# A new order of steps, loads and casts in a fused sigmoid-attention and token-mixing kernel, with more of the q/k exchange on GpSimd and idle tiled matmuls on TensorE

## The chip, the cores and the metric

The kernel runs on one core of a Trainium2 chip. The metric is device time in microseconds (us) of one execution, lower is better. A profile is one further execution recorded by the hardware profiler; its span runs from the first to the last instruction.

## The reference

Eight batches, 12 heads, sequence 448, head size 64. Sigmoid attention, then a token-mixing MLP on its output:

```python
scores = q @ k.T / sqrt(64) - log(448)        # per batch and head, 448 x 448
x = sigmoid(scores) @ v                       # heads side by side: 448 x 768 per batch
wq, wk = x @ w_q, x @ w_k                     # 448 x 64 each
W_tok = (wq @ wk.T) / sqrt(64)                # 448 x 448
out = relu(W_tok @ x) @ w_out                 # 448 x 768 per batch, float32
```

Inputs and output are float32 in device memory; the kernel computes in bf16 with float32 accumulation. It forms W_tok @ x as wq @ (wk.T @ x).

## The kernel before

**Quads.** Four heads of one batch are a quad; there are 24, three to a batch. A quad takes 7 score steps and 7 value steps. A score step (letter S, lines 299 to 310) is four 64x64-tiled matmuls into a pair of PSUM banks, then one sigmoid of 128x896 on ScalarE (line 308) which frees the pair. A value step (P or p, line 321) is four tiled matmuls into a pair that the quad keeps for all 7; after the last, VectorE (P) or ScalarE (p) copies it to `xt`. There are four bank pairs in all, handed out in the order in which they were given back.

**The MLP.** x and X transpose `xt` to `xn` on TensorE (tiled, line 361, or whole, line 344); W, w, L, l project with `w_q | w_k`: W and w as one full-array matmul (line 400), L and l as four tiled ones (line 387), whose two halves VectorE then has to copy and add (lines 394, 395); N transposes `wk`; U, u (line 431, full rows) and T, t (line 447, tiled, with an extra add at 452) form wk.T @ x; M, m form the mix and its ReLU; O, o and I, i are the output projection. Four steps make 128 rows of output. For batches 2 to 5 O is tiled (line 516); for the others O is a full-array matmul (line 600) and I its tiled form (line 556), whose halves VectorE adds (line 562).

**The order.** It is written out by hand in two strings. `PLAN` gives the steps one letter each; instructions are emitted in that order, and every engine works through its own in that order. `ORDER` gives the loads (`q7` is q of quad 7, `w3` the third row block of the output weights), issued on SP as one of six load buffers comes free, that is when the tensor six places earlier has been cast. Each is cast float32 to bf16: on GpSimd in the sequence of `ORDER`, or, where it has a dot, on VectorE, at the earliest 9 scores after its load was issued (4 in the first quads).

**How q and k get their layout.** The letter that `PLAN` gives to a quad's q sets it:

- q, k and a, b: TensorE transposes into a bank pair, VectorE copies out (lines 212, 220, 286, 291).
- c, d: the cast (line 188) writes an order in which six GpSimd copies of 32 partitions exchange quarter blocks (`arrange`, lines 157, 160, 163, one shared `swap` tile), then VectorE transposes 128 partitions, once for q and once for k (line 259).
- r, s, z: no exchange; VectorE transposes 128 partitions twice (line 252) and then four times 32 partitions (line 228, `quadrants`).
- e, f, g: exchanged as for c, plus two more VectorE transposes (line 263) and four small DMAs (line 240, `move`).

At most two quads of the c, r or e kind hold a cast buffer at once. F is a full-array matmul on zeros that nothing reads (line 814).

Of the kernel before, what the change touches and what calls it, by code (L numbers as in the profile page):

```python
# [17 lines left out]
def kernel(  # L18
# [12 lines left out]
    nc = tc.nc  # L31
    B, H, S, HD = q.shape
# [4 lines left out]
    NI, NP = 7, 64  # L37
# [4 lines left out]
    HALF = (slice(0, 64), slice(64, 128))  # L42
# [23 lines left out]
    pairs = [banks[:, 2 * n : 2 * n + 2] for n in range(4)]  # L66
    pairs16 = [banks16[:, 2 * n : 2 * n + 2] for n in range(4)]
    free2 = [0, 1, 2, 3]
# [29 lines left out]
    zeros = singles.tile([P, 512], BF16)  # L98
# [21 lines left out]
    def xt(u, j):  # L120
# [4 lines left out]


    PLAN = (
        "FSSFSKFSSqFSFSkFSpFSpSqpPpPSPSSkFSpPSFSSabSrPSPSPXSsPSPpPSpp"
        "PpSPSXSwwSSzWWXwWSPPpSPppNSPSqkSXSSpUSPSpMpSPpPSqkSSPSpPMSPP"
        "PPSSWWXSSwWWWSPpcPSdMpSPPPSXSNSxSqkSUSpPSMppSppPSOoSMSOOqSkS"  # L130
        "oOSMrPpSppPSPSPOoSSsSOzXOSCLlLSLSLLSpPPPPcpPSSdOOSOSCNxSOScU"
        "SPPSPdprPSPPSPPsPPPSpSOPSXoSxSzooSCMLlCSLllLSPcpPSPPPPSCSOdX"
        "SSOOoSMpcpSPPPPSPSONSMYOxSpPpSpSCoodSpPPSoOSxSUSLcldllSLLPSP"
        "pSPpcpPdSoSOMSoSOSXmMrPsSpPPSPoSpOSPoSoozxSoScOSSOOOSOdNSOSU"
        "SPppSMPpppPPPSpLPlSLLeppSflLOomgcOMooNOSxSoOStoSSOooeSpPdPPo"
        "PSpSPooSOfSooSSgPOoMpppSPPPOmMOSOSOSLLLlLSLSOoSOxScoOxSoSOON"
        "dPPSPPPPSSPoOSOSOSooSxoSOSTPpSPPSPppPPMPPypMpPlLMLLyLLIxiiNI"
        "IuiIMiImmIIIOooOOOOoOOoooooo"
    )
    PLAN = "".join(PLAN)  # L140
    KIND = ["a"] + [t for t in PLAN if t in "qacer"]
# [82 lines left out]
    def quadrants(n, h):  # L224
        w = pq[n].rearrange("p e t i d y -> p e (t i d y)").bitcast(F32)
        for g in range(2):
            own, other = 64 * g + 32 * h, 64 * g + 32 * (1 - h)
            nc.vector.transpose(  # L228
                out=qk[n][other : other + 32, h].rearrange("p t i n -> p (t i n)").bitcast(F32),
                in_=w[own : own + 32, 1 - h],  # L230
            )
# [3 lines left out]
    def move():  # L235
        n, m = moves.pop(0)
        for g in range(2):
            for h in range(2):
                own, other = 64 * g + 32 * h, 64 * g + 32 * (1 - h)
                nc.sync.dma_start(  # L240
                    out=qk[n][other : other + 32, h].rearrange("p t i n -> p (t i n)"), in_=m[own : own + 32, 1 - h],
                )
# [56 lines left out]
    def scores(n, i):  # L299
        fb, sc, _ = bank2()  # L300
        for g in range(2):
            for h in range(2):
                nc.tensor.matmul(  # L303
                    sc[HALF[h], g, 0:S], qk[n][HALF[g], h, 1, i, :],
                    qk[n][HALF[g], h, 0].rearrange("p i n -> p (i n)"), start=True, stop=True,
                )
        at = p_at.tile([P, 2, S], BF16, tag="at", name="at")
        nc.scalar.activation(at, sc[:, :, 0:S], ACTF.Sigmoid, bias=attn_bias, scale=attn_scale)  # L308
        release(fb)
        ats[n, i] = at  # L310
# [3 lines left out]
    def values(n, i, tail, eng):  # L314
        u, j = quads[n]
        if i == 0:
            pv[n] = bank2()
        fb, ps, _ = pv[n]
        for h in range(2):
            for g in range(2):  # L320
                nc.tensor.matmul(  # L321
                    ps[HALF[g], h, 0:S], ld["v16", n][HALF[h], i, g, :],
                    ats[n, i][HALF[h], g, :], start=(i == 0), stop=(i == NI - 1),
                )
        if i == NI - 1:
            if tail:
                for h in range(2):
                    COPY["vs"[h]](out=xt(u, j)[:, h, 0:S], in_=ps[:, h, 0:S])
            else:
                COPY[eng](out=xt(u, j)[:, :, 0:S], in_=ps[:, :, 0:S])  # L330
            release(fb)
# [80 lines left out]
    def mlp_wkn(u):  # L412
        fb, _, ps = bank1()
        for m in range(4):
            for c in range(2):
                nc.tensor.transpose(
                    ps[HALF[c], m * DH : (m + 1) * DH],
                    wqks[u % 2][HALF[1], (2 * m + c) * DH : (2 * m + c + 1) * DH],
                    ident16[HALF[1], HALF[1]],
                )  # L420
        wkn[u] = p_one.tile([P, 4, DH], BF16, tag="wkn", name="wkn")
        nc.vector.tensor_copy(out=wkn[u].rearrange("p m n -> p (m n)"), in_=ps[:, 0 : 4 * DH])
        release(fb)
# [258 lines left out]
    for n in range(7):  # L682
# [1 line left out]


    ORDER = (
        "q1 .k1 v0 q2 .k2 v1 k3 q3 q4 k4 v2 w0 v3 k5 k6 q5 "
        "v4 q6 v5 k7 v6 q7 w2 q8 q9 w1 k8 w5 v7 w3 w6 w4 "
        "k9 v8 k10 q10 k11 q11 v9 v10 .k12 q12 .k13 q13 v11 q14 k14 v12 "
        "v13 q15 k15 .q16 v14 .q17 k16 v15 .v16 k17 q18 k18 k19 v17 .k20 q19 "  # L690
        "k21 .q20 .k22 v18 q21 .k23 q22 v19 v20 .v21 v22 v23 q23 "
    )
    BY = {"s": [], "v": []}
    for x in ORDER.split():
# [55 lines left out]
    def pump():  # L750
        while pumped[0] < len(ORDER):
            nm, n = ORDER[pumped[0]]
            if (nm, n) not in OTHERS:
                if not ready(nm, n):
                    break
                cast_now(nm, n, "g")
            pumped[0] += 1
# [11 lines left out]
    def cast_by_others():  # L769
        while cast_one("s") or cast_one("v"):  # L770
            pass
# [14 lines left out]
    def tr_part(nm, t16, r, e):  # L786
        fb, _, ps = bank2()
        transposes_whole(ps[:, 0], t16, r)
        COPY[e](
            out=qk[0][:, :, "qk".index(nm), r].rearrange("p h i n -> p i h n"),  # L790
            in_=ps[:, 0, 0 : (r.stop - r.start) * P].rearrange("p (i h n) -> p i h n", h=2, n=NP),
        )
        release(fb)
# [18 lines left out]
    for t in PLAN:  # L812
        if t == "F":
            nc.tensor.matmul(pairs[free2[0]][:, 0], zeros[:, 0:P], zeros, start=True, stop=True)
            continue
        kind = ALIKE.get(t, t if t in "qkx" else t.upper())
        c = done[kind]
        done[kind] += 1
        tail = done["S"] == N * NI
        if t == "S":  # L820
            scores(*divmod(c, NI))
            cast_by_others()
        elif kind == "P":
            n, i = divmod(c, NI)
            values(n, i, tail, "s" if t == "p" else "v")
            if i == NI - 1:
                used.add(("v", n))
                pump()
        elif kind in "qk":
            if t in "rs":  # L830
                quads_r.append(c) if t == "r" else None
                if t == "s":
                    quadrants(c, 0)
            tr(c, kind, t)
            if t in "df":
                used.add(("q", c))
            if t not in "cers":
                used.add((kind, c))
                pump()
        elif t == "g":  # L840
            move()
        elif t == "z":
            n = quads_r.pop(0)
            quadrants(n, 1)
            used.update({("q", n), ("k", n)})
            pump()
        elif t == "K":
            tr_part("k", k016, K3, "v")
            tr_part("k", k016, K4, "v")
        elif kind == "x":  # L850
            tr_x(c, tail, t in "XY", "s" if t in "yY" else "v")
        elif kind == "W":
            mlp_wqk(*divmod(c, NC), tail, t in "wl", t in "Ll")
        elif kind == "C":
            for y in range(2):
                nc.sync.dma_start(out=wout16[HALF[y], NC + c, :], in_=wout16[HALF[1 - y], c, :])
        elif kind == "N":
            mlp_wkn(c)
        elif kind == "U":
            (mlp_tmp_tiled if t in "Tt" else mlp_tmp)(c, t in "ut")  # L860
        elif kind == "M":
            u, x = divmod(c, NC // 2)
            mlp_mix(u, x, t == "m", tail)
            if x == NC // 2 - 1:
                if u // 2 in TW:
                    chunks.extend((u // 2, ((u % 2, i), (u % 2, 6 - i))) for i in range(3))
                    if u % 2:
                        chunks.append((u // 2, ((0, 3), (1, 3))))
                else:
                    chunks.extend((u // 2, m, -1) for m in (range(3, NI) if u % 2 else range(3)))  # L870
        elif kind == "O":
            if (opened or chunks)[0][0] in TW:
                out_pair(t == "o")
            elif t in "Ii":
                out_halves(t == "i")
            else:
                out_chunk(t == "o", tail)
# [29 lines left out]
```

## Time and profile before

| | us |
|---|---|
| median of 3 timed runs | 189.18 (187.64 to 189.44) |
| span of the profiled execution | 187.3 |
| TensorE matmul busy | 176.1 (94%) |
| ScalarE busy | 163.6 (87%) |
| VectorE busy | 141.1 (75%) |
| GpSimd busy | 106.5 (57%) |

Busy time is the union of the instructions of an engine; a matmul lasts longer than its share of the array, because matmuls overlap, so a busy TensorE need not be full. "PEclk" is the clock that the throttle granted, in tenths of full speed. "Idle before, releaser" tells what ended the idle time of an engine just before a group of instructions.

### The profile page before, as it was taken

Reading aid. Unit: us, or ns where it says so; the run is one execution under the profiler, and the core shown is the slowest. Engines: PE = TensorE matmul, PEld = TensorE weight load, DVE = VectorE, ACT = ScalarE, POOL = GpSimd, SP = SyncE. Lnnn points to the kernel's source line nnn. Section 1 sums busy time; section 2 is a strip of 40 time slices with the busy share of each in tenths; the row PEclk is TensorE's granted clock in tenths of the full one; section 3 lists DMA queues with packets and bytes.
Section 4 is the critical chain, followed back from the end, with each engine's and each line's share of the span. In section 5 each row is a group of like instructions: output and inputs, shape, how many; then the busy total and the mean of one; then the engine's idle time right before and its main releaser. Section 6 shows DMA issues by size and latency. Waiting matters only on the chain.

```text
span 187.3 us, 8513 instructions
## 1 busy us (share of the span) xinstructions
PE 176.1 (94%) x3648; PEld 115.9 (62%) x3648; DVE 141.1 (75%) x223; ACT 163.6 (87%) x210; POOL 106.5 (57%) x145
## 2 busy tenths in 40 slices
PE   7898899989999999999999999998999999999990
PEld 7443556544555454565555776766998889786660
DVE  3354697577868999999898999977778665697810
ACT  4799999999999989999999999996999989984230
POOL 1437798972968989899999892486033900000000
PEclk9999999999999999999999999999999999999998
DMA  5999999964699989989998995984998634513395
GB/s 173 340 390 383 309 354 366 390 244 142 198 361 402 405 293 298 353 265 314 310 315 267 296 410 192 281 271 143 275 307 276 149 101 113 128 50 76 97 241 177
DMA packets 26469, 48.97 MB, mean 261 GB/s; under 512 B 4096, under 2 KB 20352, under 8 KB 26432
## 3 DMA queue, kind: packets, MB, share of 16 engines
q1 hardware_dynamic: 26272, 48.24, 79.3%
q8 instruction: 28, 0.46, 1.0%
q10 hardware_dynamic: 160, 0.20, 0.4%
q14 instruction: 9, 0.07, 0.1%
HBM read 35.78 MB, written 11.01 MB: 250 GB/s over the span
## 4 chain that ended last, share of the span: by engine, by line
PE 69%; DVE 15%; ACT 9%; issue 4%; ACTq 0%; DVEq 0%
PE banks L303 15%; PE banks L516 13%; PE banks L321 12%; PE banks L600 10%; ACT at L308 9%; DVE qk L228 4%; DVE xt L330 3%; PE banks L556 3%; PE banks L387 3%; DVE mx L459 2%; PE banks L431 2%; PE banks L361 2%; PE banks L344 2%; PE banks L677 2%; PE banks L471 1%
## 5 line engine op out<-in xcount | busy, mean ns | idle before, releaser
L308 ACT ACTIVATE at<-banks 128x896 bf16<-128x896 f32 x168 | 141.7, 927 | 5.4 <-PE banks L303 4.2
L303 PE MATMUL banks<-qk 64*64 64x448 bf16 x672 | 63.6, 359 | 4.2 <-ACT at L308 1.1
L321 PE MATMUL banks<-at,v 64*64 64x448 bf16 x672 | 46.6, 350 | 0.2
L303 PEld LDWEIGHTS <-qk 64*64 64x64 bf16 x672 | 26.0, 105 | 27.2 <-issue 16.2
L516 PE MATMUL banks<-wout,mx 64*64 64x384 bf16 x672 | 35.1, 323 | 0.0
L188 POOL CAST qk<-ld 128x896 bf16<-128x896 f32 x24 | 28.5, 1206 | 9.9 <-DVE qk L259 6.7
L198 POOL CAST v<-ld 128x896 bf16<-128x896 f32 x22 | 20.4, 931 | 15.2 <-PE banks L303 10.0
L321 PEld LDWEIGHTS <-v 64*64 64x64 bf16 x672 | 23.1, 106 | 7.8 <-issue 1.7
L516 PEld LDWEIGHTS <-mx 64*64 64x64 bf16 x672 | 24.2, 107 | 3.5
L459 DVE TENSOR_SCALAR mx<-banks 128x1024 bf16<-128x1024 f32 (+2 forms) x21 | 21.1, 1010 | 5.6 <-PE banks L483 3.3
L600 PE MATMUL banks<-wout,mx 128*128 128x384 bf16 (+1 forms) x138 | 24.7, 320 | 0.0
L330 DVE CAST xt<-banks 128x896 bf16<-128x896 f32 x20 | 21.6, 1083 | 3.7 <-PE banks L321 2.1
L600 PEld LDWEIGHTS <-mx 128*128 128x128 bf16 x138 | 11.9, 98 | 10.4 <-issue 4.5
L259 DVE STREAM_TRANSPOSE qk<-qk 128x448 f32<-128x448 f32 x24 | 15.0, 630 | 0.0
L396 POOL COPY wq<-wqk 64x448 bf16<-64x448 bf16 x6 | 3.7, 620 | 18.4 <-DVE wqk L395 18.1
L163 POOL COPY qk<-swap 32x448 uint32<-32x448 uint32 x20 | 11.8, 592 | 1.2
L525 DVE COPY o<-banks 128x768 f32<-128x768 f32 x9 | 8.6, 955 | 4.8 <-PE banks L516 4.8
L157 POOL COPY swap<-qk 32x448 uint32<-32x448 uint32 x20 | 11.1, 554 | 1.8 <-DVE qk L188 0.7
L160 POOL COPY qk<-qk 32x448 uint32<-32x448 uint32 x20 | 11.1, 554 | 1.2
L228 DVE STREAM_TRANSPOSE qk<-qk 32x448 f32<-32x448 f32 x16 | 10.2, 636 | 0.4
L374 DVE COPY xn<-banks 128x1024 bf16<-128x1024 bf16 (+1 forms) x13 | 8.2, 628 | 3.0 <-PE banks L361 1.9
L387 PE MATMUL banks<-xt,wqk 64*64 64x448 bf16 x144 | 9.9, 350 | 0.0
(94 smaller groups left out, 217.2 us busy)
## 6 DMA issues: line engine op xcount, KB each, us to landing
ld<-in_q_dram SPq DMA_DIRECT2D x24, 448.0 KB, 6.2
ld<-in_v_dram SPq DMA_DIRECT2D x24, 448.0 KB, 6.4
ld<-in_k_dram SPq DMA_DIRECT2D x23, 448.0 KB, 6.1
out_dram<-o SPq DMA_DIRECT2D x42, 192.0 KB, 4.1
ld<-in_moe_w_out_dram SPq DMA_DIRECT2D x6, 384.0 KB, 5.0
out_dram<-ld SPq DMA_DIRECT2D x11, 192.0 KB, 2.8
wout<-wout SPq DMA_DIRECT2D x12, 96.0 KB, 5.8
qk<-mv SPq DMA_DIRECT2D x8, 56.0 KB, 3.3
```

What stands on the lines that cost most here:

```text
L188: COPY[e](out=f[:, :, "qk".index(nm)].rearrange("p e i d y -> p e y i d"), in_=ld.pop((nm, n)).rearrange("p (y i e d) -> p e y i d", y=2, ...
L198: COPY[e](out=t16.rearrange("p i b d -> p b i d"), in_=ld.pop((nm, n)).rearrange("p b (i d) -> p b i d", i=NI),)
L228: nc.vector.transpose(out=qk[n][other : other + 32, h].rearrange("p t i n -> p (t i n)").bitcast(F32), in_=w[own : own + 32, 1 - h],)
L259: nc.vector.transpose(out=qk[n][:, t].rearrange("p t i n -> p (t i n)").bitcast(F32), in_=w)
L303: nc.tensor.matmul(sc[HALF[h], g, 0:S], qk[n][HALF[g], h, 1, i, :], qk[n][HALF[g], h, 0].rearrange("p i n -> p (i n)"), start=True, stop=True,
L308: nc.scalar.activation(at, sc[:, :, 0:S], ACTF.Sigmoid, bias=attn_bias, scale=attn_scale)
L321: nc.tensor.matmul(ps[HALF[g], h, 0:S], ld["v16", n][HALF[h], i, g, :], ats[n, i][HALF[h], g, :], start=(i == 0), stop=(i == NI - 1),)
L330: COPY[eng](out=xt(u, j)[:, :, 0:S], in_=ps[:, :, 0:S])
L387: nc.tensor.matmul(ps[HALF[x], y, 0:S], wqk16[HALF[y], c, 64 * x : 64 * x + 64], xt(u, c // 2)[HALF[y], c % 2, 0:S], start=(c == 0), stop= ...
L459: nc.vector.tensor_scalar(dst, ps, moe_scale, 0.0, ALU.mult, ALU.max)
L516: nc.tensor.matmul(ps[HALF[x], y, 0:NB], mx[HALF[y], u, b, 64 * (i - 3 * y) : 64 * (i - 3 * y) + 64], wout16[HALF[y], slot(y, b), x * NB : ...
L600: nc.tensor.matmul(ps, mxs[w][:, 2 * S * c + m * P : 2 * S * c + (m + 1) * P], wout16[:, c, w0:w1], start=(c == 0), stop=(c == NC - 1),)
```

## The change

No computed value changes. `PLAN` and `ORDER` are written anew, and there is one new letter, E: four tiled matmuls of 64x448 on zeros, into the pair that the next step to take one will get; nothing reads them.

```diff
     PLAN = (
-        "FSSFSKFSSqFSFSkFSpFSpSqpPpPSPSSkFSpPSFSSabSrPSPSPXSsPSPpPSpp"
-        "PpSPSXSwwSSzWWXwWSPPpSPppNSPSqkSXSSpUSPSpMpSPpPSqkSSPSpPMSPP"
...
+        "SESEEEEKSSSEFFqSEEkESFSppSPppSESPPSFFqSkPPpSpESESPPEPSSXFSqk"
+        "SSEpPEPrSESpEPPsSPWWSXSEESSzWXWWWESPPESPNpSpPPSUSESEPEESpEcd"
...
     ORDER = (
-        "q1 .k1 v0 q2 .k2 v1 k3 q3 q4 k4 v2 w0 v3 k5 k6 q5 "
-        "v4 q6 v5 k7 v6 q7 w2 q8 q9 w1 k8 w5 v7 w3 w6 w4 "
...
+        "q1 .k1 v0 v1 q2 k2 k3 v2 q3 k4 q4 w0 v3 k5 q5 .k6 .k7 v4 q6 q7 "
+        "v5 .q8 .w6 v6 k8 .w2 w1 .v8 v7 w3 .w5 w4 q9 k9 q10 k10 .q11 .k11 "
...
+        if t == "E":
+            for g in range(2):
+                for h in range(2):
+                    nc.tensor.matmul(
+                        pairs[free2[0]][HALF[h], g, 0:S], zeros[HALF[g], 0:NP], zeros[HALF[g], 0:S], start=True, stop=True,
+                    )
+            continue
```

In counts (before, after): E steps 0, 31; F steps 9, 7; quads of kind c, d 10, 17; of kind r, s, z 4, 1; of kind e, f, g 2, 0; of the TensorE kinds 8, 6 (quad 0 with them). Full-array projections W, w 12, 36; tiled ones L, l 36, 12. Output steps O, o 100, 92; I, i 12, 20. U, u 6, 4; T, t 2, 4. Steps that ScalarE finishes are fewer: lower-case o 46, 36 and m 5, 4, but i 4, 9. Casts on VectorE 12, 22. In the lines from 816 on, the numbers of the changed kernel are 7 higher.

## The prediction

> **What bounds the kernel now.** I read the stretches first, cut where the 1st, 57th, 127th and last sigmoid stand (columns: stretch, length, busy time of PE, weight load, VectorE, ScalarE, GpSimd, then clock and DMA share), then pieces of the chain of waits, the groups, and single rows of the timeline.
>
> ```profile
> 6.53:52.97 46.44, 42.41 (x882) 22.98 (x879) 31.48 (x44) 46.13 (x57) 33.72 (x42) 1.00 0.91 314
> 52.97:117.93 64.96, 64.17 (x1208) 38.18 (x1203) 60.16 (x85) 63.17 (x80) 53.81 (x71) 1.00 0.94 318
> 117.93:163.86 45.93, 45.29 (x1160) 37.20 (x1153) 34.05 (x48) 42.59 (x53) 17.04 (x23) 1.00 0.71 204
> 163.86:187.34 23.48, 18.74 (x374) 13.00 (x366) 13.06 (x27) 9.26 (x21) 0.55 (x1) 0.98 0.48 129
> ```
>
> Stage 1 (scores 1 to 56) is ScalarE's: 46.13 of 46.44 us, 0.83 us a score. In stage 2 ScalarE fills 97%, TensorE seems full, VectorE 93%. In stage 3 TensorE leads. The tail starts at the end of the last sigmoid.
>
> TensorE's busy time is inflated by overlap, so I take the price of a step from the chain:
>
> ```profile
> 165.18 0.38 PE banks L387 x8
> 138.98 0.49 PE banks L516 x12
> 173.22 1.46 PE banks L556 x36
> 174.68 6.95 PE banks L600 x42
> ```
>
> Four tiled matmuls of 448 columns take 0.19 us (the first line holds eight), an output step 0.49 (12 tiled, or 3 full: 6.95 / 14). A transpose step is 0.4 to 0.47, U 0.66, T 0.63. Multiplied by the letters of PLAN, TensorE's steps before come to 35.0, 57.1, 44.7 and 20.1 us in the four stages: spare in 1, 8 us spare in 2, full in 3 and in the tail (last matmul at 181.6, about 5 us of copies and stores behind it).
>
> ```profile
> L188 POOL CAST qk<-ld 128x896 bf16<-128x896 f32 x24 | 28.5, 1206 | 9.9 <-DVE qk L259 6.7
> L198 POOL CAST v<-ld 128x896 bf16<-128x896 f32 x22 | 20.4, 931 | 15.2 <-PE banks L303 10.0
> L163 POOL COPY qk<-swap 32x448 uint32<-32x448 uint32 x20 | 11.8, 592 | 1.2
> L157 POOL COPY swap<-qk 32x448 uint32<-32x448 uint32 x20 | 11.1, 554 | 1.8 <-DVE qk L188 0.7
> L228 DVE STREAM_TRANSPOSE qk<-qk 32x448 f32<-32x448 f32 x16 | 10.2, 636 | 0.4
> L525 DVE COPY o<-banks 128x768 f32<-128x768 f32 x9 | 8.6, 955 | 4.8 <-PE banks L516 4.8
> ```
>
> **The exchange on GpSimd.** Seven more exchanges are 14 each of lines 157, 160, 163: 14 x (0.554 + 0.554 + 0.592) = 23.8 us. Against that go 8 plain casts (7.4) and 3 of the output weights (2.5), with one line-188 cast more (1.2): GpSimd 106.5 + 15.1 = 121.6. Queued up by stage it holds 8 to 9 us more in stage 2: 62 of 65. I walked its queue with these rows, load landings spaced 1.2 us as before: quad 5 is exchanged at about 31.5 for a score due at 35, quad 7 at 39 for 47, quad 16 at 95.5 for 98; the lead stays 2 to 6 us. So it is hidden; if the lead is used up, each late exchange shows (below).
>
> **VectorE.** Gone: 12 of line 228 (7.6), net 6 of line 252 (3.7), 4 of line 263 (2.4), two bank copies (2.2), and 8 copies and adds of tiled projections (5.0, less 4 plain copies, 2.5). New: 10 of line 259 (6.3), 10 casts, the rest output copies and adds. VectorE casts took 0.67 to 1.72 us, mean about 0.9; a cast of output weights on VectorE is not in the trace, so between 0.5 (by size from 0.585, the shortest v cast) and 1.72, I take 0.7, from the undisturbed rows nearest in size. The sum over VectorE is +4, but by stage +5.8, -4.3, +1.1, +1.2.
>
> In stage 1 that falls on one place: between scores 34 and 50 VectorE's list is 13.9 us (five bank-to-`xt` or transposed copies, ReLUs, four casts, six exchange transposes and smaller ones) where it was 9.3, and 16 scores take 13.3. Back to back its instructions overlap by some 0.08 us each. Between 0 and 1.5 us; I take 0.8.
>
> **The 31 E steps.** 27 lie in stage 1, 31 x 0.19 = 5.9 us in all. The clock is 1.00 there already, so they gain none. No tiled idle step is in the trace; the nearest rows are a score's own 0.19 and an F's 0.39. An E waits for the same sigmoid as the next score, and behind it in TensorE's queue stand that score and value steps. Every E stands where 3 or 4 pairs are free to rotate: three sigmoids are 2.5 us, one turn of a pair about 1.8 (0.38 + 0.93 + waits), so 0.19 fits. Exposed are those ahead of the first quads' transposes: 0.2. From below: two F fewer gain at most 0.8; from above all 5.9. Stage 1: 46.4 + 0.8 + 0.2 = 47.4.
>
> **Loads and DMAs.** v1 now goes ahead of q2 and k2; k2's cast then ends near 15.1 instead of 13.7, and its transposes ran at 16.0, so 0. Eight moves leave SP; their quads had 5 and 10 scores of lead: 0. A VectorE cast that waits for its load holds up the copies behind it and so the banks; with 9 scores (7.5 us) after issue and 6.1 to 6.4 to land, 0.
>
> **Stage 2.** ScalarE loses 1.6 us (5.8 of copies and ReLUs to 4.1), VectorE 4.3, TensorE's steps go to 58.2. ScalarE still leads with 63.2 - 1.6, and if the stage keeps its 1.8 us above that, it takes 63.4.
>
> **Stage 3.** TensorE leads. 45 output steps become 38 (-3.4), 39 value steps 44 (+0.9), four transposes six (+0.9), and a U and an N go (-0.9): 42.3. ScalarE falls by 3.3. So 45.9 - 2.4 = 43.5. The full-array runs between tiled ones, some 0.2 us each, stay about as many (43, 42).
>
> **Tail.** 28 output steps become 32 (+2.0), value steps 10 become 5 (-0.9), a transpose goes (-0.4): +0.6. After the last mix 19 output steps follow in both, and fill covers each wait before it. More of them need a VectorE add of 0.56 us, still under their 0.98 a pair. 24.1.
>
> **The sum.** 6.5 + 47.4 + 63.4 + 43.5 + 24.1 = 184.9, against 187.3: -2.4 us. The median of the runs is 1.84 us above the profiled span; carried over, 186.8.
>
> **Rivals.** *Given back in order.* Stage 2 does not follow ScalarE: every engine there was at 93% or more and its steps are chained by a fixed order. Then it stays at 65.0: -2.4 + 1.6 = -0.8, 188.4. For it: TensorE's list in stage 2 grows by 1.1. Against: VectorE, the next in line, gets 4.3 us lighter.
>
> *GpSimd becomes the bound of stage 2.* Two casts and two copies show what happens when both engines work on SBUF:
>
> ```profile
> 66.88 1.72 DVE L188 CAST qk<-ld 128x896 bf16<-128x896 f32 x1
> 72.27 0.67 DVE L188 CAST qk<-ld 128x896 bf16<-128x896 f32 x1
> 99.75 1.17 POOL L157 COPY swap<-qk 32x448 uint32<-32x448 uint32 x2
> 96.53 1.63 POOL L163 COPY qk<-swap 32x448 uint32<-32x448 uint32 x2
> ```
>
> The 1.72 ran beside a GpSimd cast, the 1.63 (for two copies) beside two VectorE casts. With 10 exchanges in stage 2 and each pair caught once, 10 x 0.47 = 4.7; four quads whose other half VectorE casts wait 0.7 more, as line 157 did. 62.4 + 4.7 + 2.8 = 69.9 instead of 63.4: +6.5 - 2.4 = +4.1, 193.3. It decides once GpSimd's list passes 63.4 plus the lead of 4 or so that it brings into the stage; at half the price it is hidden or a wash. For it: GpSimd at 96%, VectorE casts up from 7 to 11 here. Against: that lead, and that most VectorE casts ran at 0.67 to 0.84.
>
> The Trainium skill (GPSIMD Engine Reference, Key points) says that GpSimd shares its SBUF interfaces with VectorE and contends with VectorE instructions in a two-port mode or with two SBUF inputs. The rows above agree as far as they go: only VectorE's SBUF-to-SBUF casts were seen to stretch this way. By that rule alone each of the 10 more casts costs something.
>
> *The E steps show.* If the pairs turn slower than I think, half of the 5 us in stage 1 would show: +2.3, 189.1; the trace has scores only 0.2 to 0.4 us ahead of their sigmoids at some quad starts. Against it is the free third pair.
>
> **Chances.** Forecast 0.46; given back 0.22; E steps show 0.10; GpSimd 0.22. A measurement here can tell about 1% (1.9 us) from no change. Faster by over 1% (below 187.3): 0.46, nearly all the forecast's; within 1%: 0.28, given back, E steps and little of the forecast's upper end going against partial stalls; slower (above 191.1): 0.26, GpSimd's case and stalls that add up. The forecast alone spans 185.0 (no stall in stage 1, a full gain in stage 2) to 187.8. The range goes from 184.6 up to 192.0, short of the full price of the last case.
>
> **What would show it.** Right: sigmoids 1 to 56 within 47.6 us; ScalarE busy near 159; stage 3 near 43.5; GpSimd waiting, not waited for; line 259 rarely idle before on GpSimd. Wrong: VectorE's transposes or scores idle behind lines 160 and 163; VectorE casts well above 0.9 us; idle time of ScalarE at scores 35 to 50; scores idle behind E; a gap in TensorE after the last score.

## The result and the profile after

The changed kernel takes 196.25 us (median of 4 runs, 194.09 to 197.42), the kernel before in the same session 189.07: a ratio of 1.036, 95% interval 1.031 to 1.042. It is slower; the forecast was 186.8. The profiled execution took 196.73 us, with a span of 194.8. Ratios leave out executions well above the others of the same kernel; the profiled ones of e6 and e9 below are of that kind (199.40 and 199.13 us), so their stages tell the place of a wait and not its size. The stretches, cut at the same sigmoids as before (same columns):

```profile
6.38:55.68 49.30, 44.93 (x903) 25.75 (x901) 36.06 (x52) 46.73 (x56) 36.93 (x49) 1.00 0.90 310
55.68:123.13 67.45, 64.45 (x1246) 37.88 (x1242) 57.60 (x78) 63.00 (x77) 60.24 (x83) 1.00 0.86 290
123.13:169.57 46.44, 43.76 (x1114) 33.28 (x1106) 34.97 (x45) 40.10 (x48) 26.30 (x38) 1.00 0.64 188
169.57:194.83 25.26, 19.70 (x450) 13.82 (x442) 15.03 (x29) 9.58 (x20) 0.55 (x1) 0.97 0.56 143
```

No stretch is shorter than before: +2.9, +2.5, +0.5 and +1.8 us. In stage 2 every engine but GpSimd has idle time that it did not have: TensorE 3.0 us (0.8 before), ScalarE 4.5 (1.8), VectorE 9.9 (4.8). The work itself went about where the diff sends it; what is new is waiting. Groups of the pages say where, first two of the kernel before, then those of the changed kernel:

```profile
L308 ACT ACTIVATE at<-banks 128x896 bf16<-128x896 f32 x168 | 141.7, 927 | 5.4 <-PE banks L303 4.2
...
L321 PE MATMUL banks<-at,v 64*64 64x448 bf16 x672 | 46.6, 350 | 0.2
```

```profile
L308 ACT ACTIVATE at<-banks 128x896 bf16<-128x896 f32 x168 | 143.0, 925 | 12.6 <-PE banks L303 10.6
...
L321 PE MATMUL banks<-at,v 64*64 64x448 bf16 x672 | 48.1, 351 | 4.3 <-POOL v L198 3.2
...
L188 POOL CAST qk<-ld 128x896 bf16<-128x896 f32 x25 | 30.6, 1243 | 8.9 <-DMA ld<-in_k_dram 4.9
...
L163 POOL COPY qk<-swap 32x448 uint32<-32x448 uint32 x34 | 20.3, 598 | 2.0
...
L160 POOL COPY qk<-qk 32x448 uint32<-32x448 uint32 x34 | 19.9, 587 | 2.0
L157 POOL COPY swap<-qk 32x448 uint32<-32x448 uint32 x34 | 19.3, 568 | 2.7 <-DVE qk L188 0.7
L198 POOL CAST v<-ld 128x896 bf16<-128x896 f32 x18 | 17.2, 964 | 3.7 <-DMA ld<-in_v_dram 2.8
```

The sigmoids (L308) waited 12.6 us, most of it for scores (5.4 before). The value steps (L321) waited 4.3 us, 3.2 of it for a cast of v on GpSimd; before it was 0.2 in all. GpSimd's own casts of v waited 15.2 us before, 10.0 of it for TensorE's work: they ran ahead. Now they wait 3.7, and 2.8 of it for loads: that lead is gone.

The longest such wait, on GpSimd and then on TensorE (start, duration; in brackets the idle time before and what ended it):

```profile
122.84 1.16 POOL L163 COPY qk<-swap 32x448 uint32<-32x448 uint32 x2
124.06 1.20 POOL L188 CAST qk<-ld 128x896 bf16<-128x896 f32 x1
125.32 1.17 POOL L157 COPY swap<-qk 32x448 uint32<-32x448 uint32 x2
126.55 1.17 POOL L160 COPY qk<-qk 32x448 uint32<-32x448 uint32 x2
127.77 1.16 POOL L163 COPY qk<-swap 32x448 uint32<-32x448 uint32 x2
129.00 1.26 POOL L198 CAST v<-ld 128x896 bf16<-128x896 f32 x1
```

```profile
127.92 0.38 PE L303 MATMUL banks<-qk 64*64 64x448 bf16 x4
130.31 0.38 PE L321 MATMUL banks<-at,v 64*64 64x448 bf16 x4 [2.01 <-POOL v L198]
```

GpSimd works back to back, and the cast of v18 that TensorE needs stands behind the exchanges of quads 19 and 20, whose turn comes later: 2.01 us. At 52.6 us the cast of v7 does the same (0.83 us).

The chain of waits in stage 1 shows how such a delay feeds itself (pieces in order of time: start, length, what). Below it stand a line of SP's waits (in total, times, longest) and a row of GpSimd:

```profile
35.65 1.32 DVE qk L188
...
37.90 5.35 DMA ld<-in_k_dram
43.26 0.05 issue
43.31 1.19 POOL qk L188
44.50 2.14 issue
...
51.66 0.93 POOL v L198
```

```profile
SPq L651 <- DVE qk L188: 4.5, 1, 4.5
```

```profile
46.66 0.83 POOL L737 CAST wout<-ld 128x768 bf16<-128x768 f32 x1 [2.16 <-DMA ld<-in_moe_w_out_dram]
```

A cast of k7, which the change moves from GpSimd to VectorE, ends at 36.97 and frees a load buffer. SP had stood 4.5 us before this cast; from 36.99 it issues the loads that had queued up, at 37.90 the one of k8, which takes 5.35 us to land. GpSimd casts it at 43.31, waits 2.16 us more for a load of output weights that came in the same burst (the piece "issue"), exchanges quad 8 and reaches v7 at 51.66. As a load is issued when the tensor six places earlier has been cast, a late cast makes a late load, and that makes the next cast late.

### The profile page after: what moved, and what is told of

Same layout as the page of the kernel before. It is cut to its first block, busy times and chain, and to the rows that moved or that the text cites. A ratio compares the mean times of both kernels' runs of the same rounds, so it can differ in the third digit from the quotient of the medians.

```text
span 194.8 us, 8713 instructions
## 1 busy us (share of the span) xinstructions
PE 178.1 (91%) x3734; PEld 115.6 (59%) x3736; DVE 146.3 (75%) x225; ACT 161.9 (83%) x204; POOL 125.5 (64%) x177
## 4 chain that ended last, share of the span: by engine, by line
PE 57%; ACT 10%; POOL 9%; DMA 7%; DVE 7%; issue 6%; ACTq 0%; POOLq 0%; DVEq 0%
PE banks L516 13%; PE banks L303 10%; PE banks L321 10%; ACT at L308 9%; PE banks L600 6%; DMA ld<-in_k_dram 5%; PE banks L556 5%; POOL qk L163 2%; DMA out_dram<-o 2%; PE banks L361 2%; PE banks L677 2%; DVE v L198 2%; POOL v L198 2%; POOL swap L157 2%; DVE qk L259 1%
## 5 line engine op out<-in xcount | busy, mean ns | idle before, releaser
L308 ACT ACTIVATE at<-banks 128x896 bf16<-128x896 f32 x168 | 143.0, 925 | 12.6 <-PE banks L303 10.6
L321 PE MATMUL banks<-at,v 64*64 64x448 bf16 x672 | 48.1, 351 | 4.3 <-POOL v L198 3.2
L188 POOL CAST qk<-ld 128x896 bf16<-128x896 f32 x25 | 30.6, 1243 | 8.9 <-DMA ld<-in_k_dram 4.9
L321 PEld LDWEIGHTS <-v 64*64 64x64 bf16 x672 | 21.6, 106 | 12.8 <-POOL v L198 4.0
L600 PE MATMUL banks<-wout,mx 128*128 128x384 bf16 (+1 forms) x114 | 21.7, 319 | 0.0
L163 POOL COPY qk<-swap 32x448 uint32<-32x448 uint32 x34 | 20.3, 598 | 2.0
L259 DVE STREAM_TRANSPOSE qk<-qk 128x448 f32<-128x448 f32 x34 | 21.1, 629 | 0.6 <-POOL qk L163 0.6
L160 POOL COPY qk<-qk 32x448 uint32<-32x448 uint32 x34 | 19.9, 587 | 2.0
L157 POOL COPY swap<-qk 32x448 uint32<-32x448 uint32 x34 | 19.3, 568 | 2.7 <-DVE qk L188 0.7
L198 POOL CAST v<-ld 128x896 bf16<-128x896 f32 x18 | 17.2, 964 | 3.7 <-DMA ld<-in_v_dram 2.8
L600 PEld LDWEIGHTS <-mx 128*128 128x128 bf16 x114 | 9.5, 98 | 9.5 <-issue 5.3
L396 POOL COPY wq<-wqk 64x448 bf16<-64x448 bf16 x2 | 1.1, 553 | 19.7 <-DVE wqk L395 19.7
L188 DVE CAST qk<-ld 128x896 bf16<-128x896 f32 x11 | 10.0, 911 | 3.2 <-DMA ld<-in_k_dram 2.6
L819 PE MATMUL banks<-zeros 64*64 64x448 bf16 x124 | 10.6, 355 | 0.7 <-DVE xt L330 0.4
```

What stands on the lines that cost most here:

```text
L157: eng.tensor_copy(out=z[lo], in_=w[hi, 0])
L163: eng.tensor_copy(out=w[lo, 1], in_=z[lo])
L188: COPY[e](out=f[:, :, "qk".index(nm)].rearrange("p e i d y -> p e y i d"), in_=ld.pop((nm, n)).rearrange("p (y i e d) -> p e y i d", y=2, ...
L198: COPY[e](out=t16.rearrange("p i b d -> p b i d"), in_=ld.pop((nm, n)).rearrange("p b (i d) -> p b i d", i=NI),)
L259: nc.vector.transpose(out=qk[n][:, t].rearrange("p t i n -> p (t i n)").bitcast(F32), in_=w)
L321: nc.tensor.matmul(ps[HALF[g], h, 0:S], ld["v16", n][HALF[h], i, g, :], ats[n, i][HALF[h], g, :], start=(i == 0), stop=(i == NI - 1),)
```

## The experiments

My theory after this, called G: GpSimd's queue, which is worked off in order, is what became late, because the further exchanges stand in it between the loads and the casts of v. Rivals: the loads come late, because load buffers are held too long (L), by the ten further casts on VectorE above all (V); the E steps take TensorE's time (E); the exchanges cost by contention, not by their place; the order itself loses elsewhere. The table gives each run's ratio to the kernel before (a point below is 0.01 of it, 1.9 us) and the stages of its profiled execution; the edits follow. In e2, e11, e12, e13 and e17 the copies of some quads are left out, so their q and k reach the heads in the wrong layout; all other work is done.

| run | ratio, 95% interval | stage 1, 2, 3, tail (us) |
|---|---|---|
| before | 1 | 46.4, 65.0, 45.9, 23.5 |
| changed | 1.036 (1.031 to 1.042) | 49.3, 67.5, 46.4, 25.3 |
| e1 no E | 1.043 (1.039 to 1.048) | 48.4, 66.5, 47.8, 25.1 |
| e2 five exchanges left out | 1.016 (1.012 to 1.021) | 48.7, 64.9, 44.2, 25.0 |
| e3 five quads back on VectorE | 1.091 (1.083 to 1.099) | 49.1, 71.3, 50.5, 25.1 |
| e4 eight load buffers | 1.065 (1.058 to 1.073) | 50.4, 72.9, 43.3, 25.2 |
| e5 the same, weight moves early | 1.061 (1.051 to 1.071) | 48.4, 74.0, 44.1, 24.9 |
| e6 two v casts ahead | 1.031 (1.021 to 1.041) | 50.5, 70.9, 44.4, 25.2 |
| e7 VectorE casts after 6 scores | 1.058 (1.049 to 1.068) | 51.3, 68.7, 46.9, 25.1 |
| e8 before, eight buffers | 1.006 (1.001 to 1.010) | 47.0, 65.7, 45.4, 23.4 |
| e9 before, five exchanges | 1.043 (1.035 to 1.050) | 46.4, 73.3, 47.0, 23.5 |
| e10 before, three exchanges | 1.007 (1.003 to 1.011) | 46.4, 67.0, 45.0, 23.5 |
| e11 e2 without E | 1.015 (1.008 to 1.021) | 50.0, 65.0, 43.9, 25.0 |
| e12 e2, ten casts back on GpSimd | 1.039 (1.033 to 1.045) | 49.8, 69.4, 44.2, 25.1 |
| e13 seven exchanges left out | 1.018 (1.012 to 1.024) | 47.8, 65.7, 44.2, 25.3 |
| e14 tail with O for I | 1.041 (1.036 to 1.046) | 48.9, 66.9, 49.3, 24.7 |
| e15 before, two exchanges | 1.005 (1.001 to 1.009) | 46.4, 64.9, 45.9, 23.3 |
| e16 e15 with full projections | 1.015 (1.011 to 1.019) | 46.7, 66.1, 46.4, 23.6 |
| e17 e2 without ten E | 1.015 (1.010 to 1.021) | 47.1, 65.0, 45.3, 25.2 |
| e18 changed without ten E | 1.031 (1.024 to 1.038) | 47.6, 67.4, 46.4, 25.4 |

**e1, no E steps.**

```diff
-        "SESEEEEKSSSEFFqSEEkESFSppSPppSESPPSFFqSkPPpSpESESPPEPSSXFSqk"
+        "SSKSSSFFqSkSFSppSPppSSPPSFFqSkPPpSpSSPPPSSXFSqkSSpPPrSSpPPsS"
...
```

> The changed kernel without its 31 E steps, all else as it is. Theory E (idle steps delay the first quads): stage 1 (49.3 us to the 57th sigmoid, 46.4 before the change) goes back by 1 to 2 us, ratio to before 1.026 to 1.031 instead of 1.036. Theories G (GpSimd's queue is the bound) and L (loads come late): within 0.4 us of the changed kernel, ratio 1.034 to 1.038.

Without E it is no faster: the E steps as a whole aren't the cause. Stage 1 got 0.9 us shorter in this execution and stage 3 1.4 longer, with a stall of 2.14 us for the same cast of v18 and 3.41 us at half clock behind it (see the end).

**e2, the copies of quads 10, 13, 18, 20 and 22 left out.**

```diff
-        if KIND[n] in "er":
+        if KIND[n] in "er" or n in (10, 13, 18, 20, 22):
             return
```

> The changed kernel without the six GpSimd copies of quads 10, 13, 18, 20 and 22 (this part of the computation is left out; the casts and VectorE's transposes stay). GpSimd loses 5 x 3.4 = 17 us, VectorE nothing. Theory G: values no longer wait for v casts behind exchanges, 4 to 6 us less, ratio 1.005 to 1.016. Theory L: the load buffers are held by casts on VectorE, which stay; at most 1.5 us less, ratio 1.028 or more. Theory E: no change.

```profile
6.69:55.42 48.73, 45.10 (x903) 25.95 (x901) 36.81 (x52) 46.44 (x56) 38.28 (x49) 1.00 0.91 312
55.42:120.31 64.89, 64.01 (x1246) 38.10 (x1242) 56.96 (x78) 62.43 (x78) 51.66 (x68) 1.00 0.92 308
120.31:164.48 44.17, 43.41 (x1113) 33.27 (x1106) 34.72 (x45) 39.79 (x48) 16.88 (x23) 1.00 0.65 189
164.48:189.50 25.02, 19.70 (x450) 13.82 (x442) 15.02 (x29) 9.60 (x21) 0.56 (x1) 0.96 0.58 144
```

These are e2's stretches. GpSimd has 8.6 us less in stage 2 and 9.4 less in stage 3, nothing else is taken away, and the kernel gains 2.0 points of ratio (3.8 us), most of it in stages 2 and 3; stage 1, where no copy is missing, still has a wait of 1.65 us for v7. So the five exchanges are rather more than half of the loss, and the rest lies elsewhere.

**e3, the same five quads exchanged by VectorE again** (10, 13, 18 as r, s, z; 20 and 22 as e, f, g).

```diff
...
-        "cpSpSPOdOSpSpPESEqkSOoSMSoOSPPpSSPppPSOOSESSWcoWoWdWSMSWOWxS"
+        "cpSpSPOdOSpSpPESEqkSOoSMSoOSPPpSSPppPSOOSESSWroWoWszWSMSWOWx"
...
```

> The changed kernel with quads 10, 13, 18 taken by VectorE's 32-partition transposes (r, s and z, z directly behind s) and quads 20, 22 by the extra transposes and DMAs (e, f, g), as before the change. GpSimd loses 17 us, VectorE gains 3 x 2.5 + 2 x 1.3 = 10 us, 7.5 of them in stage 2, where it has 57.5 of 67.5. Theory G: 2 to 4 us less, ratio 1.015 to 1.026. Theory L: nothing gained, and VectorE's longer list delays its casts and so the loads: ratio 1.036 to 1.05.

```profile
55.66:126.98 71.32, 65.29 (x1246) 38.47 (x1242) 64.55 (x90) 62.76 (x78) 50.87 (x67) 1.00 0.83 272
```

This missed what both theories expected. VectorE's work in stage 2 is up 7.0 us on the changed kernel's, GpSimd's down 9.4, and the stage takes 71.3 us; the three longest waits of TensorE there (1.50, 1.88, 1.60 us) are for ReLUs and copies on VectorE. In stage 3 it waits 2.73 us for the small DMAs of an e quad. In the changed order, with ten more casts on VectorE, the transposes can't simply go back there.

**e9, e10, e15: five, three and two of those quads given to GpSimd in the kernel before,** by letters alone (e15: 20 and 22; e10: 18 too; e9: 10 and 13 too; the lines shown are e15's).

```diff
...
-        "SPppSMPpppPPPSpLPlSLLeppSflLOomgcOMooNOSxSoOStoSSOooeSpPdPPo"
+        "SPppSMPpppPPPSpLPlSLLcppSdlLOomcOMooNOSxSoOStoSSOoocSpPdPPoP"
...
```

> One part of the change done alone: the kernel before, with quads 10, 13 and 18 exchanged by GpSimd (r, s, z become c, d) and quads 20 and 22 too (e, f, g become c, d). GpSimd gains 17 us, 10 of them in stage 2, where it had 53.8 of 65.0; VectorE loses 10 us, 7.5 of them there, where it had 60.2. Theory G: GpSimd then fills 64 of 65 us and its casts come late, 2 to 5 us more, ratio 1.01 to 1.027. Rival (the exchange is cheap, the changed kernel's own order is at fault): VectorE's relief wins, ratio 0.985 to 1.0.

> The kernel before with quads 18, 20 and 22 alone exchanged by GpSimd, in whose places it stood idle (5.9 us at 114, 5.9 at 130, 4.1 at 139). Theory G: the copies fit into that idle time, VectorE loses 5 us beside a TensorE that leads: ratio 0.99 to 1.002. Rival: the waits there are of casts that now come later still: ratio 1.005 to 1.02.

> The kernel before with quads 20 and 22 alone exchanged by GpSimd (c and d for e, f, g), where GpSimd was nearly free. Theory G (an exchange costs nothing where GpSimd's queue has room, and spares VectorE four transposes and SP eight small transfers): 0.993 to 1.000, the stage of TensorE 45.0 to 45.5 us as with three quads, the second stage back at 65.0 (67.0 with three). Rival (any further exchange stretches VectorE's casts beside it): 1.003 to 1.010.

```profile
70.31 1.52 PE L321 MATMUL banks<-at,v 64*64 64x448 bf16 x28 [1.88 <-POOL v L198]
83.21 0.38 PE L303 MATMUL banks<-qk 64*64 64x448 bf16 x4 [2.60 <-DVE xt L330]
```

```profile
81.53 0.65 DVE L259 STREAM_TRANSPOSE qk<-qk 128x448 f32<-128x448 f32 x1 [3.60 <-POOL qk L160]
```

The rows are e9's, TensorE and then VectorE. Five exchanges alone, with the order, loads and casts as they were, cost as much as the whole change (1.043; G had expected 1.027 at most), with the mark of the changed kernel, a value step that waits 1.88 us for a v cast on GpSimd, and one that the changed kernel doesn't have: VectorE sits 3.60 us in front of a transpose whose copies are late, with TensorE's scores behind it. VectorE has less to do there than before (55.19 us against 60.16 in stage 2). Contention is small here: GpSimd is busy for 124.4 us, and 106.5 before plus ten more of each copy at the means of before (17.0) makes 123.5, so 0.9 us is all that its instructions were stretched by. Three exchanges, two of them in stage 3 where GpSimd was busy for 37%, cost 0.7%: stage 2 +2.0, stage 3 -1.0. In stage 2 a cast of q on VectorE stands 2.40 us before its load lands, and TensorE 2.67 us behind it. Two cost 0.5% (0.1 to 0.9); the profiled span, 186.9 against 187.3, shows no place for it. Both ratios fall into the bands of the rivals, not of G, which had expected no loss where GpSimd has room. The mechanism of e15's rival, stretched casts, isn't seen: VectorE's casts of lines 188 and 198 took 10.3 us in all, as before. So an exchange that VectorE is spared gains nothing here even where GpSimd is free (VectorE's work in stage 3 falls from 34.1 to 31.9 us, the stage stays at 45.9), and where GpSimd is full it costs several us.

**e12, e2 with ten casts moved from VectorE back to GpSimd** (and v7 one place ahead, v15 four).

```diff
...
-        "v5 .q8 .w6 v6 k8 .w2 w1 .v8 v7 w3 .w5 w4 q9 k9 q10 k10 .q11 .k11 "
...
+        "v4 q6 q7 v5 .q8 w6 v6 k8 w2 w1 v7 v8 w3 w5 w4 q9 k9 "
...
```

> The changed kernel without the copies of quads 10, 13, 18, 20, 22 (left out) and with ten casts taken from VectorE to GpSimd (three of the output weights, v8, v9, v12, v13, v15, q11, q12), so that VectorE casts 12, as before the change. GpSimd has room for their 9 us. Theory V (VectorE's casts wait for landings in front of the copies that free banks, and hold load buffers): 1.5 to 3 us less than with the copies alone left out, ratio 1.0 to 1.008. Rival: GpSimd gets late again, ratio 1.016 or more.

```profile
POOL v L198 <- DMA ld<-in_v_dram: 10.3, 6, 5.7
```

This line of e12's waits says: GpSimd's v casts waited six times for their loads, 10.3 us in total and 5.7 at the longest (5.2 us in e2). GpSimd is busy for 55.8 of stage 2's 69.4 us, so it isn't full; it is late because its queue stands still at a load that was issued late. That loses 2.3 points on e2, so it doesn't help to hand these ten casts back. It doesn't show that casts on VectorE are free: k7, the cast that held SP for 4.5 us in the chain above, stays on VectorE in e12, and no run moves it alone.

**e6, v7 and v18 cast earlier.**

```diff
...
-        "v5 .q8 .w6 v6 k8 .w2 w1 .v8 v7 w3 .w5 w4 q9 k9 q10 k10 .q11 .k11 "
...
+        "v4 q6 q7 v5 .q8 .w6 v6 v7 k8 .w2 w1 .v8 w3 .w5 w4 q9 k9 "
...
```

> The changed kernel with v7 cast before k8 and v18 before k19 and q19, so that neither stands behind the GpSimd exchange of the next quads; the loads swap places with the casts. Theory G: TensorE's waits of 0.8 us at score 54 and 2.0 us at score 132 for these casts go, and 2 to 3 us with them: ratio 1.021 to 1.027. If the lateness only moves to the exchanges that now come later (GpSimd is full, whatever the order): within 1 us, ratio 1.031 to 1.04.

1.031, within the error of 1.036. The two waits shown above went; in the profiled execution a VectorE cast of k (line 188) that waited 3.6 us for its load and a gap of 2.87 us at score 99 came instead. Moving the late cast ahead seems only to choose which one is late.

**e4, e5, e7, e8: attempts to open the loop of load buffers.** e4 has eight instead of six; e5 also moves the output weights' SBUF-to-SBUF DMAs (letter C) behind score 58; e7 lets VectorE's casts come 6 scores after the load instead of 9; e8 is e5's edit on the kernel before.

```diff
-    lds = [singles.tile([P, 2 * NI * HD], F32, name=f"ld{n}") for n in range(6)]
+    lds = [singles.tile([P, 2 * NI * HD], F32, name=f"ld{n}") for n in range(8)]
...
-            if len(ring) >= 6 and ring[-6] not in cast:
+            if len(ring) >= 8 and ring[-8] not in cast:
```

```diff
-    LAG = 9
+    LAG = 6
```

> The changed kernel with eight load buffers instead of six, so that a load waits for the cast eight places earlier. Theory L: GpSimd's and VectorE's waits for landings (some 13 us together behind the first casts) go, and quads 7, 11, 15, 17 come back to 6 to 6.5 us: 2 to 4 us less, ratio 1.015 to 1.026. Theory G: at most 1 us, ratio 1.031 to 1.037. Theory E: no change.

> Eight load buffers as in the run before, and the six C steps (twelve SBUF-to-SBUF DMAs that copy the halves of the output weights, all on SP) moved together behind score 58. With eight buffers alone, TensorE stood 5.3 us before line 516 for these DMAs, which lay on SP behind loads that waited for casts, and the clock was halved for 3.4 us after it. If that stall alone hid the gain of the buffers (theory L): 5.3 + 1.7 = 7 us less than with eight buffers alone, about 193.4, ratio 1.024. If more buffers do not help (theory G alone): as the changed kernel, ratio 1.032 to 1.04.

> The changed kernel with VectorE's casts allowed 6 scores after their load was issued instead of 9; the order of steps is the same. Theory L: buffers come free up to 2.5 us earlier and loads with them, 1 to 2 us less, ratio 1.026 to 1.031. Rival: a load takes 6.2 us to land and 6 scores are 5 us, so VectorE stands in front of casts whose data has not landed, and copies behind them come late: ratio 1.04 or more.

> The kernel before the change with eight load buffers and its six C steps behind score 58. If loads were on its path too: 1 to 3 us less, ratio 0.985 to 0.995. If its casts kept up with six buffers, as its few waits for landings say (VectorE 0, GpSimd some 4 us in the steady part): 0.997 to 1.003.

A row of TensorE in e4, then one of VectorE and one of TensorE in e5:

```profile
117.70 2.52 PE L516 MATMUL banks<-wout,mx 64*64 64x384 bf16 x26 [5.33 <-DMA wout<-wout]
```

```profile
72.00 1.05 DVE L198 CAST v<-ld 128x896 bf16<-128x896 f32 x1 [4.76 <-DMA ld<-in_v_dram]
```

```profile
74.10 0.59 PE L303 MATMUL banks<-qk 64*64 64x448 bf16 x4 [6.09 <-DVE mx L459]
```

More buffers do free the value steps of late v casts (idle before line 321: 0.2 us in e4, 4.3 in the changed kernel), and stage 3 comes down to 43.3. But SP issues in order too: in e4 the weights' DMAs stood behind loads, 5.33 us of TensorE. In e5 a VectorE cast, placed nine scores after its load's turn in the program, came to its turn 4.76 us before the load had landed; MLP copies queued behind it and TensorE waited 6.09 us. In e7 VectorE's casts waited for landings as well (3.7 us). In the kernel before, more buffers gain nothing (1.006): its loads were no limit. All three are slower than the changed kernel, where L had expected a gain: each way to mend the loop put the wait into another queue. That the loop is part of the cause is argued from what went and what came; no version without it was found.

**e13, two more exchanges left out (quads 5 and 8).**

```diff
-        if KIND[n] in "er":
+        if KIND[n] in "er" or n in (5, 8, 10, 13, 18, 20, 22):
             return
```

> The changed kernel without the GpSimd copies of quads 5 and 8 as well as 10, 13, 18, 20, 22: q and k of these seven quads reach their heads in the wrong layout. Theory G (what is left over the forecast in the first stage comes from exchanges 5 and 8 standing in GpSimd's queue ahead of the cast of v7): quad 7 goes from 8.0 back to about 6 us, the first stage from 48.7 to about 47, ratio to the kernel before about 1.006 where five quads left out gave 1.016. Rival (the rest is the order of the steps itself, or VectorE's longer list there): first stage stays at 48.5 or more, ratio 1.014 to 1.018.

Quad 7 came back from 8.03 us to 6.38, as G said, but the ratio did not move: quad 8 went from 6.25 to 7.48. In e13's row of TensorE

```profile
57.01 0.41 PE L212 MATMUL banks<-ident,k 64*64 64x64 bf16 x28 [0.71 <-POOL k L198]
```

the next cast on GpSimd, k of a TensorE quad, is the one waited for. The mechanism at quad 7 is G's; that it was worth 2 us was wrong. e13 leaves out the copies of all seven quads that the change newly exchanges and is still at 1.018: the other half of the loss doesn't come from these copies.

**e11, e17, e18: the E steps again.** e11 is e2 without any E, e17 e2 without the ten between scores 13 and 28, e18 the changed kernel without those ten.

```diff
-        "SESEEEEKSSSEFFqSEEkESFSppSPppSESPPSFFqSkPPpSpESESPPEPSSXFSqk"
-        "SSEpPEPrSESpEPPsSPWWSXSEESSzWXWWWESPPESPNpSpPPSUSESEPEESpEcd"
+        "SESEEEEKSSSEFFqSEEkESFSppSPppSESPPSFFqSkPPpSpSSPPPSSXFSqkSSp"
+        "PPrSSpPPsSPWWSXSSSzWXWWWSPPESPNpSpPPSUSESEPEESpEcdSMPPpPSPSX"
...
```

> The changed kernel without the copies of quads 10, 13, 18, 20, 22 (left out, as above) and without its 31 E steps. Without the 2 us stall at score 132 there is nothing that halves the clock. Theory E: 1 to 2 us less than with the copies alone left out (ratio 1.016), ratio 1.006 to 1.011. Rival (E steps are hidden, as the prediction has it): ratio 1.014 to 1.018.

> The kernel that leaves out five exchanges (their q and k reach the heads in the wrong layout), and in addition without the ten E steps between scores 13 and 28; the other 21 stay. If these ten delay quad 2's last value step, its copy to xt and so the bank pair that the fourth score of quad 3 waits for (0.93 us, quad 3 taking 6.8 us where a kernel with no E took 5.6): quad 3 goes to 5.6 to 5.8 us, the first stage from 48.7 to 47.6, the ratio from 1.016 to about 1.010. Rival (the first stage's loss is given back at the next late v cast, as 0.9 us at quad 7 was at quad 8): quad 3 as said, but ratio 1.014 to 1.018 again. Second rival (the E steps cost nothing): quad 3 stays at 6.7 or more.

> The changed kernel, all exchanges kept, without the same ten E steps between scores 13 and 28. If GpSimd's queue sets the time, a quad 3 that is 1.1 us shorter only lets GpSimd fall further behind its scores: first stage 48.2 to 49.3, ratio 1.032 to 1.040, no better than with all E steps. If TensorE's fuller list early is what makes the loads and casts late: ratio 1.030 or less.

Quads 2 and 3 together take 11.6 us before, 13.0 in the changed kernel, 11.2 in e17 and e18. In the changed kernel TensorE waits 0.93 us at score 24 (27.06 us) for a sigmoid to free its bank pair; without the ten steps that wait is 0.27. But e2, with all E steps, did not have it either (its quads 2 and 3 took 11.4 us, so that the 6.8 that I expected there was e13's): it comes in some executions only. e17 has the shortest stage 1 of all (47.1) and the same ratio as e2, since stage 3 gave 1.1 us back. e18's ratio is half a point under the changed kernel's, which the intervals don't separate. With E steps quads 2 and 3 can take 1.8 us longer, and little or nothing of that reaches the end. Without any of them e11's profiled execution ran 6.83 us of the first stage at half clock, after a stall of 2.04 us; e1's did not.

**e14, e16: the tail and the projections.**

```diff
-        "LLPPmPLOPOOMMoLLLyIiIyNiOtoOoMmiMiiIiIIiIiIIIIiIOoOO"
+        "LLPPmPLOPOOMMoLLLyIiIyNiOtoOoMmiMiiIiIIiIiIIOoOoOoOO"
```

```diff
...
-        "oOSMrPpSppPSPSPOoSSsSOzXOSCLlLSLSLLSpPPPPcpPSSdOOSOSCNxSOScU"
+        "oOSMrPpSppPSPSPOoSSsSOzXOSCWWWSWSWWSpPPPPcpPSSdOOSOSCNxSOScU"
...
```

> The changed kernel with the last block of the tiled output projection (four I steps) written as O steps, so that VectorE has no adds and SP fewer stores in the last microseconds. If the stores that SP still issues after the data are ready make the end late: the tail goes from 25.1 to 24.3 to 24.6 us, the whole ratio from 1.036 to about 1.032. If it is only that TensorE has more steps there: 24.9 to 25.2, ratio as before. Stages 1 to 3 as in the changed kernel under both.

> The kernel before with quads 20 and 22 exchanged by GpSimd and every tiled projection ahead of the last score written as a full-array one (W for L and l): VectorE loses a copy and an add for each, ScalarE the copy of each l. If TensorE's and VectorE's sums carry over where GpSimd isn't late: VectorE's 3 to 4 us less gain 0.5 to 1.5 us, ratio 0.987 to 0.996. If the switches between tiled and full matmuls (0.2 us each, some 10 more) count instead: 1.000 to 1.010.

e14's tail is 0.5 us shorter than the changed kernel's, less than expected from the stores, and the other runs of the changed order spread from 24.9 to 25.4 with no edit there. Its stage 3 is 2.9 us longer, with a stall of 2.63 us for v18 (2.01 in the changed kernel) and 3.41 us at half clock behind it, which the edit doesn't touch, so that the ratio says nothing on the tail. For e16, TensorE's rows around two projection steps, in e15 (tiled) and in e16 (full):

```profile
125.15 0.36 PE L303 MATMUL banks<-qk 64*64 64x448 bf16 x4
125.34 0.55 PE L387 MATMUL banks<-xt,wqk 64*64 64x448 bf16 x8
125.72 0.55 PE L321 MATMUL banks<-at,v 64*64 64x448 bf16 x8
```

```profile
126.24 0.38 PE L303 MATMUL banks<-qk 64*64 64x448 bf16 x4
126.56 0.55 PE L400 MATMUL banks<-xt,wqk 128*128 128x448 bf16 x2
127.04 0.57 PE L321 MATMUL banks<-at,v 64*64 64x448 bf16 x8
```

From start to start it is 0.19 and 0.38 us tiled, 0.32 and 0.48 full: in these rows a full-array run between tiled matmuls costs 0.23 us of switching. e16 has 13 such runs more than e15 (55 against 42), which makes an estimate of 3.0 us, and is 1.0 point slower (2.0 us), although VectorE has 3.6 us less to do. The changed kernel has 43 runs: there the projections stand together with other full-array steps, and by this count the switches are no part of its loss.

## Why the prediction was wrong

- **The failing step** is the one under the exchange on GpSimd: "I walked its queue with these rows, load landings spaced 1.2 us as before", "the lead stays 2 to 6 us. So it is hidden". The sum was near: 121.6 forecast, 125.5 measured, and 60.2 us against 62 in stage 2. The exchanges themselves were hidden as forecast: in the changed kernel quad 5's ended at 31.5 us, as walked, and each one 3.8 us or more ahead of its quad's first sigmoid; VectorE's transposes (line 259) waited 0.6 us for the copies in all. But the lead was compared with the scores alone. The walk gives no time for the casts of v that stand behind the exchanges in the same queue, and TensorE waited for those (2.01 us for v18, 0.83 for v7); and it took the landings as given, although a load is issued only when a buffer is cast free. e2 (2.0 points back) and e9 (a loss of the same size from five exchanges alone) show that the exchanges on GpSimd cost rather more than half of what was lost; e12 (the same loss again from ten casts in their place) shows that other work in that queue costs as much. e4, e5 and e7 point to the buffers in the loop, by what the wait turned into, without settling it.
- **The rival "GpSimd becomes the bound"** had the right engine and, at 193.3 us, too small a price. It priced contention. That came: GpSimd's means rose from 1206 to 1243 (line 188), 931 to 964 (v, line 198), 554 to 568, 554 to 587 and 592 to 598 ns (lines 157, 160, 163), in all 25 x 0.037 + 18 x 0.033 + 34 x (0.014 + 0.033 + 0.006) = 3.3 us over the whole span, and VectorE's casts of v took 1.18 us on average (six) where the two before took 0.80. But the larger price is the waiting in order. The Trainium skill (GPSIMD Engine Reference, Key points) has GpSimd contend with VectorE instructions in a two-port mode or with two SBUF inputs; the longer means agree as far as they go, but no run here shows in which mode these casts run. Its point of decision, GpSimd's list against the stage's time plus its lead, was wrong too: e12 is late with GpSimd busy for 80% of stage 2.
- **Loads: a VectorE cast that waits for its load was put at 0.** The casts of line 188 on VectorE waited 3.2 us in all:

```profile
91.49 0.67 DVE L188 CAST qk<-ld 128x896 bf16<-128x896 f32 x1
94.02 0.91 DVE L188 CAST qk<-ld 128x896 bf16<-128x896 f32 x1 [1.86 <-DMA ld<-in_k_dram]
```

  The "9 scores (7.5 us) after issue" of the estimate are counted in the program; the load itself was issued later, when its buffer came free. The casts on VectorE held up the loads in turn (SP's 4.5 us above), which has no term in the sum.
- **Stage 1, 47.4 forecast, 49.3 measured.** VectorE's list between scores 34 and 50, which I gave 0.8 us, cost about 0.2 (from the 34th to the 50th sigmoid 13.1 us before, 13.3 after). The E steps were given 0.2; quads 2 and 3 are 1.5 us longer than before, and without E they are not (nor in e2, with all E): the pairs can turn more slowly there than "so 0.19 fits" says. Quad 7 (5.8 to 7.2 us) is the late v7, not in the sum at all.
- **Stage 2, 63.4.** With the exchanges out of the way (e2) it takes 64.9, which is the rival "given back in order" (65.0): ScalarE's work fell by 0.7 us instead of 1.6, VectorE's by 3.2 instead of 4.3, and the stage followed neither. (That rival's "every engine there was at 93% or more" leaves out GpSimd, at 53.8 of 65.0 us, 83%.) Which step of the order holds it there was not settled.
- **Stage 3, 43.5.** The sum of TensorE's step prices was right to 0.7 us: 43.9 to 44.2 in e2, e11, e12 and e13, without the exchanges (45.3 in e17). The changed kernel's other 2.3 us come with them.
- **Tail, 24.1 forecast, 25.3 measured.** From the last sigmoid to the end of the last matmul it is 19.7 us (18.7 before), +1.0 for the forecast 0.6; from there to the end 5.6 (4.7 before), forecast as unchanged. In e14, one block without adds, the latter is 5.0, but it is 5.3 in e2 and 5.7 in e18 with no edit there; the rest is open. (The last matmul before ended at 182.6; the prediction's 181.6 is the end of a piece of the chain.)
- **The forecast 185.0 to 187.8 was not reached by any run of the changed order.** Of the 9.9 us between the forecast span (184.9) and the measured 194.8, e2 puts 5.3 on the five exchanges (3.8 by the ratios); the rest, in e2, is stage 1 (+1.3), stage 2 given back (+1.5), stage 3 (+0.7), tail (+0.9) and 0.2 in the head. e13 and e17 show that to mend the part of stage 1 alone brings no time.

## What to carry to other kernels

When work is moved to an engine with idle time, don't compare sums: walk everything that stands behind the moved work in that engine's queue up to the instruction that waits for it, and close the loop if that engine also frees the buffers that its own loads need. An engine that is 57% busy may have no room where it is 83% busy for a third of the kernel. A wait that an edit removes is only gained when the next queue in order isn't late as well. Test a part of a change by putting it alone into the old kernel, and by taking it alone out of the new one.

## What was not expected of the hardware

After stalls that are short against the kernel, TensorE's granted clock falls to half. e5's stretches around its 6.09 us stall (clock in the third column from the end):

```profile
68.00:74.00 6.00, 0.01 (x2) 0.00 (x0) 2.00 (x3) 0.21 (x1) 4.27 (x7) 0.89 0.90 285
74.00:81.00 7.00, 6.90 (x71) 2.87 (x71) 5.03 (x9) 4.52 (x5) 1.97 (x3) 0.60 0.99 321
81.00:90.00 9.00, 9.00 (x155) 4.46 (x153) 7.13 (x11) 8.86 (x12) 6.27 (x10) 1.00 0.67 240
```

The records of the clock give 6.83 us at 0.5 there. They give 6.83 us also after a stall of 2.04 us (e11), and 3.41 us after stalls of 1.89 us (e7), 2.14 (e1), 2.63 (e14), 2.73 (e3), 2.87 (e6), 3.04 (e9) and 5.33 us (e4). They give none after the changed kernel's 2.01 us, nor after 2.23 (e12), 2.60 (e9), 2.67 (e10) and 3.09 us (e7). So the length of a stall alone doesn't decide it.

All these pieces are multiples of 3.41 us, and they begin on a grid of 3.41 us. Counted by the windows of that grid, all five windows with matmuls missing for 2.07 us or more were followed by half clock. Of the six with 1.85 to 2.01 us two were (e6, e7) and four were not, so the point lies near there, a little above half a window; e7's 3.09 us fall as 1.5 and 1.6 on two windows. Two windows with 1.56 us (e3, e11) that were followed by half clock don't fit. The Trainium skill (TensorE: Matmul & The Clock Gate, "What's actually happening") has a free-running window of 3413 ns, which agrees, and half clock after at least one idle window of about 3.4 us, which doesn't: here less was enough. A late cast thus costs its wait and sometimes, by an estimate from these records, up to 1.7 us (half of 3.41) of TensorE's work on top.
